# Chunked attention and a gated feed-forward block on one core: the query spread moves from GpSimd to VectorE, and GpSimd's loads get a small wait of their own

## The chip, the cores and the metric

The kernel runs on one core of a Trainium2 chip. The metric is the device time of one launch in microseconds, as the median of several runs. Four runs of the kernel before gave 236.3, 235.44, 234.52 and 234.93 us, median 235.18 us.

A core has five engines with instruction streams of their own: TensorE (PE in the profile) multiplies matrices into PSUM banks, VectorE (DVE) and ScalarE (ACT) do elementwise work, GpSimd (POOL) does elementwise work too and issues transfers, and SyncE (SP) issues transfers. Every stream runs in program order; an instruction that waits holds up all that stand behind it on its engine.

## The reference

Sequences of 768 tokens, 4 batches, 8 heads of 64. Each chunk of 32 queries attends to 8 memory rows, 16 keys to the left of the chunk, its own 32 and 8 to the right. Then a gated feed-forward layer over all 3072 tokens.

```python
for c in range(nc):                                   # 24 chunks of 32
    k_full = concat([mem_k, k[:, :, l_start:r_end]])  # up to 8 + 56 rows
    v_full = concat([mem_v, v[:, :, l_start:r_end]])
    a = softmax(scale * q_c @ k_full.T)
    out[:, :, c_start:c_end] = a @ v_full
x = out.transpose(0, 2, 1, 3).reshape(B * S, H * D)   # 3072 x 512
y = (maximum(x @ w_gate, 0) * (x @ w_val)) @ w_out    # 512 -> 1536 -> 512
```

## The kernel before

The tokens are worked in 8 blocks of 384 (`NB = 8`, `TB = 384`; block n is half a sequence). For a block there are two kinds of work.

**Attention, per pair of heads** (`hp`, 4 pairs, each 128 partitions wide). `score` (L282 for blocks 2 and later) multiplies the transposed keys `kT` with `qbd`, in which the transposed queries `qT` of the two heads of a pair are laid out block-diagonally: the two halves are copied into place and the rest stays zero. `score_exp` (L294) takes three exponentials on ScalarE. `step_v` (L344) multiplies with the value windows; `step_ln` (L350, two logarithms) and `step_e` (L355, one exponential) give the reciprocal of the row sums on ScalarE; `step_m` (L361, two multiplications on VectorE) writes the pair's part of `xT`.

**The feed-forward layer** of a block is 15 units: 12 inner units (`ffn_unit`, 4 matmuls into a bank `g_ps`, 4 into `v_ps`, L382; then a relu on ScalarE, L390, and a multiplication on VectorE, L394, after which the two banks are free) and 3 out units (`out_unit`, 12 matmuls into `o_ps`, L418; ScalarE copies the result and issues its store from block 2 on). Four PSUM banks (`fps`) go round among `g_ps`, `v_ps` and `o_ps`; so the units can run two ahead of the elementwise work. The scores have one buffer (`sps`), and `step_v` has one pair of banks (`xo_ps`, `xs_ps`).

`run(n, at)` is one round. It walks through the 15 units u of block n - 1 and puts block n's attention in between: pair hp's score goes behind unit `at[hp]`, its `step_v` and `step_ln` into the middle of unit `at[hp] + 2` with `step_e` behind that unit, and `step_m` ahead of unit `at[hp] + 3`. The list is (0, 3, 6, 9), but (3, 5, 8, 11) in the first round, which is `run(3)`. In `run(3)` units 0 and 1 are opened together (chunks). Everything is issued in the order written; there is no scheduler.

**Where the inputs come from.** For each block from 2 on, `loads(n)` has GpSimd issue 4 transfers for the key band, 4 for the queries (`q16n`) and 4 for the value band; SyncE copies the memory rows. SyncE then issues two transposing transfers, `turn_k_dma` (L233, `kT`) and `turn_q_dma` (L238, `qT`). Then `spread_q` (L246) makes `qbd` out of `qT` by four copies: two of 64 x 384 (pair 0, the two halves) and two of 64 x 1152 (pairs 1 to 3). `qbds` has two buffers, and so have `kT`, `qT`, `k16s`, `vwins` and `q16n`.

**Who does the spread, before.** For block 2 it is VectorE, ahead of the six out units in `run1()`. For block 3 it is GpSimd, in `run1()` behind the fourth of the six out units; for blocks 4 to 7 it is GpSimd too, issued in `run(n)` at u = 9 right behind the transposes. As `loads(n + 2)` stands behind `spread_q(n + 1)` in GpSimd's stream, the loads wait for that block's query transpose and for the four copies.

`gate` is a tile of 128 x 1. It is written once in the kernel before, by a GpSimd copy from `kTs[2]`, so that the loads of block 3, which stand behind it, wait for block 2's key transpose.

Of the kernel before, what the change touches and what calls it, by code (L numbers as in the profile page):

```python
# [17 lines left out]
def kernel(  # L18
# [12 lines left out]
    nc = tc.nc  # L31
# [5 lines left out]
    HP = H // 2  # L37
# [4 lines left out]
    NB = B * S // TB  # L42
    NQ = 4
# [7 lines left out]
    NDC = DFF // 128  # L51
    NT = TB // 128
# [20 lines left out]
    dve_copy, act_copy = nc.vector.tensor_copy, nc.scalar.copy  # L73
# [10 lines left out]
    qbds = [const.tile([128, NQ, HP, 2, QB], F16, name=f"qbd{p}") for p in range(2)]  # L84
# [12 lines left out]
    gate = const.tile([128, 1], F16, name="gate")  # L97
# [42 lines left out]
    def load_band(n, src_t, dsts):  # L140
        b, p = divmod(n, 2)
        for i in range(NQ):
            m0, m1 = (16 if (p == 0 and i == 0) else 0), (112 if (p == 1 and i == NQ - 1) else BAND)
            src = bass.AP(tensor=src_t.tensor, offset=src_t[b, 0, TB * p + QB * i - 16 + m0, 0].offset,
                          ap=[[D, m1 - m0], [S * D, H], [1, D]])
            pool_dma(dsts[p][NMEM + m0:NMEM + m1, i, :, 0:D], src)  # L146
# [6 lines left out]
    def load_mem_k(n):  # L153
        b, p = divmod(n, 2)
        m = memk[:, H * b:H * b + H, :]
        src = bass.AP(tensor=m.tensor, offset=m.offset, ap=[m.ap[0], [0, NQ], [1, H * D]])
        sp(k16s[p][0:NMEM].rearrange("m i h d -> m i (h d)"), src)

    def load_mem_v(n):
        b, p = divmod(n, 2)  # L160
        for i in range(NQ):
            sp(vwins[p][0:NMEM, i, :, 0:D], memv[:, H * b:H * b + H, :])
# [3 lines left out]
    def load_q_tokens(n):  # L166
        b, p = divmod(n, 2)
        q16s[n] = half.tile([QB, NQ, H, D], F16, tag="q16", name="q16n")
        for i in range(NQ):
            src = bass.AP(tensor=q.tensor, offset=q[b, 0, TB * p + QB * i, 0].offset,  # L170
                          ap=[[D, QB], [S * D, H], [1, D]])
            pool_dma(q16s[n][:, i], src)  # L172
# [6 lines left out]
    kTs, qTs = {}, {}  # L179
# [51 lines left out]
    def turn_k_dma(n):  # L231
        kTs[n] = turned.tile([128, NQ, HP, 128], F16, tag="kT", name="kT")
        nc.sync.dma_start_transpose(kTs[n].rearrange("p i a m -> p (i a) m"),  # L233
                                    k16s[n % 2].rearrange("p i h d -> p (i h d)"))

    def turn_q_dma(n):
        qTs[n] = turned.tile([128, NQ, HP, QB], F16, tag="qT", name="qT")
        nc.sync.dma_start_transpose(qTs[n].rearrange("p i a m -> p (i a) m"),  # L238
                                    q16s[n].rearrange("p i h d -> p (i h d)"))

    def spread_q(n, copy=nc.gpsimd.tensor_copy):

        for a in (slice(0, 1), slice(1, HP)):
            for hh in range(2):
                s = slice(D * hh, D * hh + D)
                copy(qbds[n % 2][s, :, a, hh, :], qTs[n][s, :, a, :])  # L246


    exs, lns, rinvs, xTs = {}, {}, {}, {}
# [108 lines left out]
    def step_m(n, hp):  # L358
        rinv = rinvs.pop((n, hp))
        for hh in range(2):  # L360
            nc.vector.tensor_tensor(out=x_of(n)[D * hh:D * hh + D, hp, :], in0=vbanks[n, hp][hh][0:D],  # L361
                                    in1=rinv[:, hh, :], op=ALU.mult)
# [5 lines left out]
    def ffn_open(n, ms, spare=False):  # L368
        if ms[0] == 0:
            gvs[n] = gpool.tile([128, NDC, TB], F16, name="gv")  # L370
        units[n] = []
        for m in ms:
            if spare:
                sc = pools["s"].tile([128, 2, 512], F32, tag="sc", name="gv_ps")
                pair = sc[:, 0, 0:TB], sc[:, 1, 0:TB]
            else:
                pair = bank("g_ps")[:, 0:TB], bank("v_ps")[:, 0:TB]
            units[n].append((pair, m))
# [17 lines left out]
    def ffn_close(n):  # L396
        for x in range(len(units[n])):
            ffn_relu(n, x)
            ffn_mult(n, x)
# [11 lines left out]
    def out_unit(n, t, between=()):  # L411
        o_ps = bank("o_ps")
        last = n == NB - 1 and t == NT - 1
        for m in range(NDC):
            if m == NDC // 2:
                for piece in between:
                    piece()
            nc.tensor.matmul(o_ps, lhsT=gvs[n][:, m, 128 * t:128 * t + 128], rhs=wo[:, m, :],  # L418
                             start=(m == 0), stop=(m == NDC - 1))
        o_sb = opool.tile([128, DM], F32, name="o_sb")  # L420
        row0 = TB * n + 128 * t
        if last:
            for s, copy, dma in ((slice(0, 256), dve_copy, sp), (slice(256, 512), act_copy, act_dma)):
                copy(o_sb[:, s], o_ps[:, s])
                dma(out[row0:row0 + 128, s], o_sb[:, s])
        elif n < 2:
            dve_copy(o_sb, o_ps)
            sp(out[row0:row0 + 128, :], o_sb)
        else:
            nc.scalar.copy(o_sb, o_ps)  # L430
            act_dma(out[row0:row0 + 128, :], o_sb)

    def unit(n, u, between=()):
        if u < NDC:
            ffn_unit(n, u, between)
        else:
            out_unit(n, u - NDC, between)
# [80 lines left out]
    def chunk(n, f):  # L518
        for x in range(2):
            for a in range(2):  # L520
                ffn_mm(n, x, f, a)
# [161 lines left out]
    def pieces(n, what):  # L683
        for w, hp in what:
            STEP[w](n, hp)
# [3 lines left out]
    def run(n, at):  # L689
        for u in range(NDC + NT):  # L690
            if n < NB:
                pieces(n, [("m", hp) for hp in range(HP) if u == at[hp] + 3])
            now = [hp for hp in range(HP) if n < NB and u == at[hp] + 2]
            inner, outer = ("ve", "") if u >= NDC else ("v", "e")
            if n == 3 and u < 2:

                if u == 0:
                    ffn_open(2, (0, 1))
                    for f in range(NFC):
                        chunk(2, f)  # L700
                    ffn_close(2)
            else:
                unit(n - 1, u, [lambda w=(w, hp): pieces(n, [w]) for hp in now for w in inner])
            pieces(n, [(w, hp) for hp in now for w in outer])
            if n < NB:
                pieces(n, [("s", hp) for hp in range(HP) if u == at[hp]])
            if u == 9 and n + 1 < NB:
                turn_k_dma(n + 1)
                turn_q_dma(n + 1)
                spread_q(n + 1)  # L710

    def pair2(hp):
        if hp < HP:
            score(2, hp)
        if hp > 0:
            step_v(2, hp - 1)
        if hp > 1:
            step_m(2, hp - 2)  # L720
        if hp < HP:
            score_exp(2, hp)
        if hp > 0:
            step_ln(2, hp - 1)
            step_e(2, hp - 1)

    def run1():
        for u in range(NDC):
            unit(1, u)
            if u < len(clear):  # L730
                clear[u]()
        spread_q(2, dve_copy)
        for t in range(2 * NT):
            out_unit(t // NT, t % NT, [lambda: pair2(t - 1)] if t > 0 else [])
            if t == 1:
                turn_k_dma(3)
            if t == 2:
                turn_q_dma(3)
            if t == 3:
                spread_q(3)  # L740
        step_m(2, HP - 1)

    def loads(n):
        if n < NB:
            load_mem_k(n)
            load_band(n, k, k16s)
            load_q_tokens(n)
            load_band(n, v, vwins)
            load_mem_v(n)


    nc.gpsimd.tensor_copy(gate, kTs[2][:, NQ - 1, HP - 1, 0:1])
    loads(3)
    run1()
    for n in range(2, NB):
        loads(n + 2)
        run(n + 1, (3, 5, 8, 11) if n == 2 else (0, 3, 6, 9))
# [1 line left out]
_INS = ['q', 'k', 'v', 'mem_k', 'mem_v', 'moe_w_gate', 'moe_w_val', 'moe_w_out']  # L759
_OUTS = [((3072, 512), 'float32')]  # L760
# [25 lines left out]
```

## Time and profile before

| what | value |
|---|---|
| median of four runs | 235.18 us (234.52 to 236.3) |
| device time of the profiled execution | 236.3 us |
| span of the profiled execution, first to last instruction | 234.3 us |
| granted TensorE clock, mean | 1.000 |
| TensorE matmuls busy | 225.9 us, 96% of the span |
| ScalarE, VectorE, GpSimd busy | 139.3, 110.7, 103.5 us |
| start-up until the first long chain of matmuls | some 25 us, bound by weight loads |
| six out units of blocks 0 and 1 with block 2's attention (`run1`) | 56.5 to 74.5 us |
| `run(3)`: block 2's units, block 3's attention | 74.5 to 101.9 us |
| `run(4)`, `run(5)`, `run(6)`, `run(7)`, then block 7's units | from 101.9, 128.6, 154.7, 180.7, 206.7 us |

The stages' bounds are the starts of the first matmuls of each block in the timeline of TensorE. In a row of the timeline the first two columns are the start and the duration of what is merged in the row, in microseconds; behind them stand the engine, the line, the operation, what it writes and reads, and the number of instructions; a bracket gives how long the engine was idle before, and what released it. Matmuls overlap: four with 384 columns are shown as 0.81 us long, while the next four start 0.65 us after them.

### The profile page before, as it was taken

What the parts mean: (1) busy time and instruction counts of PE and PEld (TensorE: products, weight loads), DVE (VectorE), ACT (ScalarE), POOL (GpSimd) and SP (SyncE); (2) the same over time, 40 slices, a digit from 0 to 9 for tenths busy, and PEclk for the clock granted to TensorE, in tenths of its full rate; (3) what the DMA queues carried; (4) which work ended last, traced back from release to release, by engine and by line L of the source; (5) the groups of instructions that cost most, each with busy time, mean ns of one, the idle gap of its engine ahead of it and who ended that gap; (6) DMA issues with size and microseconds to landing.
All of it is one profiled execution on the core that took longest, in us unless ns stands there. A gap on an engine that the chain in (4) does not pass through costs nothing.

```text
span 234.3 us, 4593 instructions
## 1 busy us (share of the span) xinstructions
PE 225.9 (96%) x1727; PEld 131.1 (56%) x1727; DVE 110.7 (47%) x214; ACT 139.3 (59%) x294; POOL 103.5 (44%) x140
## 2 busy tenths in 40 slices
PE   7999899999999999999999999999999999999993
PEld 3655455665554666446654666456654666456541
DVE  4685647883546445225461266215560365214300
ACT  3483793342397488657882798458873898433420
POOL 8778766431950598049803990795050000000000
PEclk9999999999999999999999999999999999999999
DMA  7999999999999899969998999299902100120012
GB/s 166 172 195 196 196 191 207 162 123 158 129 159 153 237 73 134 150 178 67 140 144 147 104 139 178 71 139 174 171 0 90 45 3 0 45 92 0 0 46 91
DMA packets 110144, 28.47 MB, mean 122 GB/s; under 512 B 93882, under 2 KB 107178, under 8 KB 110122
## 3 DMA queue, kind: packets, MB, share of 16 engines
q0 software_dynamic: 81760, 15.13, 81.1%
q1 hardware_dynamic: 25354, 8.07, 22.6%
q10 hardware_dynamic: 3008, 4.98, 6.0%
q8 instruction: 13, 0.21, 0.3%
q14 instruction: 9, 0.07, 0.1%
HBM read 31.08 MB, written 6.29 MB: 160 GB/s over the span
## 4 chain that ended last, share of the span: by engine, by line
PE 72%; DMA 19%; POOL 4%; ACT 1%; issue 1%; DVE 0%; SPq 0%; POOLq 0%
PE v_ps L382 22%; PE g_ps L382 22%; PE o_ps L418 20%; DMA qT<-q16n 7%; DMA wg<-in_moe_w_gate_dram 3%; DMA wv<-in_moe_w_val_dram 3%; DMA rk<-in_k_dram 3%; PE sc_ps L282 3%; DMA q16n<-in_q_dram 2%; POOL qbd L246 2%; POOL k L146 1%; PE xo_ps L344 1%; PE xs_ps L344 1%; POOL q16n L172 1%; ACT ex L294 1%
## 5 line engine op out<-in xcount | busy, mean ns | idle before, releaser
L394 DVE TENSOR_TENSOR gv<-v_ps,gr 128x384 f16<-128x384 f32 x95 | 52.5, 555 | 83.9 <-ACT gr L390 68.5
L382 PE MATMUL v_ps<-xT,wv 128*128 128x384 f16 x380 | 79.1, 326 | 0.8 <-DMA wv<-in_moe_w_val_dram 0.5
L382 PE MATMUL g_ps<-xT,wg 128*128 128x384 f16 x380 | 79.3, 326 | 0.3 <-DMA wg<-in_moe_w_gate_dram 0.2
L418 PE MATMUL o_ps<-wo,gv 128*128 128x512 f16 x288 | 64.3, 379 | 0.0
L390 ACT ACTIVATE gr<-g_ps 128x384 f16<-128x384 f32 x95 | 46.2, 489 | 28.9 <-PE g_ps L382 15.7
L382 PEld LDWEIGHTS <-wg 128*128 128x128 f16 x384 | 36.7, 98 | 23.8 <-issue 1.1
L382 PEld LDWEIGHTS <-wv 128*128 128x128 f16 x384 | 36.1, 98 | 22.9 <-DMA wv<-in_moe_w_val_dram 0.9
L418 PEld LDWEIGHTS <-gv 128*128 128x128 f16 x288 | 27.9, 98 | 31.7
L294 ACT ACTIVATE ex<-sc_ps,bias 128x256 f16<-128x256 f32 x84 | 33.4, 469 | 10.8 <-PE sc_ps L282 7.6
L246 POOL COPY qbd<-qT 64x384 f16<-64x384 f16 (+1 forms) x20 | 16.5, 825 | 48.4 <-DMA qT<-q16n 47.5
L430 ACT COPY o_sb<-o_ps 128x512 f32<-128x512 f32 x17 | 10.0, 586 | 27.9 <-PE o_ps L418 17.8
L146 POOL DMA_DIRECT2D k<-in_k_dram x24 | 21.5, 904 | 2.4 <-DMA wv<-in_moe_w_val_dram 1.0
L355 ACT ACTIVATE rinv<-ln,mln 64x768 f32<-64x768 f32 x24 | 22.2, 925 | 0.2
L146 POOL DMA_DIRECT2D vwin<-in_v_dram x24 | 21.5, 904 | 0.5 <-DVE gv L394 0.3
L172 POOL DMA_DIRECT2D q16n<-in_q_dram x24 | 18.5, 778 | 3.5 <-DMA wo<-in_moe_w_out_dram 3.5
L361 DVE TENSOR_TENSOR xT<-xo_ps,rinv 64x384 f16<-64x384 f32 x24 | 13.2, 550 | 11.7 <-ACT rinv L355 11.7
L350 ACT ACTIVATE ln<-xo_ps 64x384 f32<-64x384 f32 x24 | 11.7, 487 | 11.8 <-PE xs_ps L344 11.7
L361 DVE TENSOR_TENSOR xT<-xs_ps,rinv 64x384 f16<-64x384 f32 x24 | 13.2, 551 | 0.7
L344 PEld LDWEIGHTS <-vwin 128*128 128x128 f16 x192 | 10.8, 98 | 3.5 <-issue 0.4
L282 PE MATMUL sc_ps<-qbd,kT 128*128 128x192 f16 x96 | 11.8, 246 | 0.5 <-POOL qbd L246 0.5
L344 PE MATMUL xo_ps<-ex,vwin 128*128 128x96 f16 x96 | 11.1, 206 | 0.4 <-ACT ex L294 0.4
L350 ACT ACTIVATE ln<-xs_ps 64x384 f32<-64x384 f32 x24 | 11.4, 474 | 0.0
(92 smaller groups left out, 136.0 us busy)
## 6 DMA issues: line engine op xcount, KB each, us to landing
out_dram<-o_sb ACTq DMA_DIRECT2D x17, 256.0 KB
q16n<-in_q_dram POOLq DMA_DIRECT2D x24, 96.0 KB, 4.8
k<-in_k_dram POOLq DMA_DIRECT2D x18, 120.0 KB, 4.0
vwin<-in_v_dram POOLq DMA_DIRECT2D x18, 120.0 KB, 7.6
wg<-in_moe_w_gate_dram POOLq DMA_DIRECT2D x6, 256.0 KB, 8.1
wv<-in_moe_w_val_dram POOLq DMA_DIRECT2D x6, 256.0 KB, 8.9
wo<-in_moe_w_out_dram POOLq DMA_DIRECT2D x3, 512.0 KB, 10.8
out_dram<-o_sb SPq DMA_DIRECT2D x6, 256.0 KB
```

Of the source, the lines that this page charges most:

```text
L146: pool_dma(dsts[p][NMEM + m0:NMEM + m1, i, :, 0:D], src)
L172: pool_dma(q16s[n][:, i], src)
L246: copy(qbds[n % 2][s, :, a, hh, :], qTs[n][s, :, a, :])
L294: nc.scalar.activation(flat[:, :, :, s], view[:, :, :, s], ACT.Exp, scale=SCALE, bias=(bias1 if n == 1 else bias)[:, g:g + 1])
L344: nc.tensor.matmul((xo, xs)[hh][:, QB * i:QB * i + QB], lhsT=vw[:, i, 2 * hp + hh, :], rhs=ex[:, hh, i, :], start=True, stop=True)
L350: nc.scalar.activation(ln[:, hh], vbanks[n, hp][hh][D:128], ACT.Ln, scale=1.0 / 64.0)
L355: nc.scalar.activation(rinv, lns.pop((n, hp)), ACT.Exp, scale=-1.0, bias=mln64[0:D, :])
L361: nc.vector.tensor_tensor(out=x_of(n)[D * hh:D * hh + D, hp, :], in0=vbanks[n, hp][hh][0:D], in1=rinv[:, hh, :], op=ALU.mult)
L382: nc.tensor.matmul(ps[a], lhsT=(wg, wv)[a][:, f, 128 * m:128 * m + 128], rhs=xTs[n][:, f, :], start=(f == 0), stop=(f == NFC - 1))
L390: nc.scalar.activation(grs[n, m], g_ps, ACT.Relu)
L394: nc.vector.tensor_tensor(out=gvs[n][:, m, :], in0=v_ps, in1=grs.pop((n, m)), op=ALU.mult)
L418: nc.tensor.matmul(o_ps, lhsT=gvs[n][:, m, 128 * t:128 * t + 128], rhs=wo[:, m, :], start=(m == 0), stop=(m == NDC - 1))
```

## The change

VectorE does every spread. For block 3 it stands behind unit 3 of `run(3)`; for blocks 4 to 7 behind the last out unit (u = 14) of the round. Ahead of `loads(n + 2)` GpSimd gets a copy of one column of `qTs[n + 1]` into `gate`. In `run(3)` block 3's scores go behind units 4, 7, 9 and 11; `step_v`, `step_e` and `step_m` follow from that by the same offsets.

```diff
-    def spread_q(n, copy=nc.gpsimd.tensor_copy):
+    def spread_q(n):
         for a in (slice(0, 1), slice(1, HP)):
             for hh in range(2):
                 s = slice(D * hh, D * hh + D)
-                copy(qbds[n % 2][s, :, a, hh, :], qTs[n][s, :, a, :])
+                dve_copy(qbds[n % 2][s, :, a, hh, :], qTs[n][s, :, a, :])
...
             if u == 9 and n + 1 < NB:
                 turn_k_dma(n + 1)
                 turn_q_dma(n + 1)
+
+            if n == 3 and u == 3:
+                spread_q(3)
+            if u == NDC + NT - 1 and n + 1 < NB:
                 spread_q(n + 1)
...
-        spread_q(2, dve_copy)
+        spread_q(2)
...
             if t == 2:
                 turn_q_dma(3)
-            if t == 3:
-                spread_q(3)
...
     for n in range(2, NB):
+        if n + 2 < NB:
+            nc.gpsimd.tensor_copy(gate, qTs[n + 1][:, NQ - 1, HP - 1, 0:1])
         loads(n + 2)
-        run(n + 1, (3, 5, 8, 11) if n == 2 else (0, 3, 6, 9))
+        run(n + 1, (4, 7, 9, 11) if n == 2 else (0, 3, 6, 9))
```

## The prediction

> **What bounds the kernel now.** I read the page's busy times first, then the waits of TensorE, then the timelines of the stage that the change touches.
>
> ```profile
> span 234.3 us, 4593 instructions
> PE 225.9 (96%) x1727; PEld 131.1 (56%) x1727; DVE 110.7 (47%) x214; ACT 139.3 (59%) x294; POOL 103.5 (44%) x140
> ...
> PE sc_ps L282 <- POOL qbd L246: 0.5, 1, 0.5
> ...
> PE xo_ps L344 <- ACT ex L294: 0.4, 1, 0.4
> ```
>
> TensorE is busy for 225.9 of 234.3 us at a granted clock of 1.000, and the chain of waits is plain matmuls from 103.8 us to the end. The reader is to see how little TensorE waits: in the part that the change can reach there are two waits, one for GpSimd's `qbd` and one for an exponential. A gain can come from those two alone. Their true price is read from starts in TensorE's timeline, since four matmuls of 384 columns are followed 0.65 us after their start:
>
> ```profile
> 79.77 0.81 PE L382 MATMUL v_ps<-xT,wv 128*128 128x384 f16 x4
> 80.42 0.49 PE L282 MATMUL sc_ps<-qbd,kT 128*128 128x192 f16 x4
> 80.75 0.81 PE L382 MATMUL g_ps<-xT,wg 128*128 128x384 f16 x4
> ...
> 85.32 0.81 PE L382 MATMUL g_ps<-xT,wg 128*128 128x384 f16 x4
> 86.53 0.20 PE L344 MATMUL xo_ps<-ex,vwin 128*128 128x96 f16 x1 [0.40 <-ACT ex L294]
> ...
> 102.52 0.81 PE L382 MATMUL v_ps<-xT,wv 128*128 128x384 f16 x4
> 103.84 0.49 PE L282 MATMUL sc_ps<-qbd,kT 128*128 128x192 f16 x4 [0.52 <-POOL qbd L246]
> ```
>
> The value step of pair 1 could have started at 85.32 + 0.65 = 85.97 and started at 86.53: 0.56 us lost. Block 4's first score could have started at 103.17 and did at 103.84: 0.67 us lost. Together 1.23 us, 0.5% of the span. The same rows give the sizes used below: half a unit 0.65, a unit 1.30, a score 0.33 us; a value step takes 0.34 and an out unit 2.59 us by their starts.
>
> **The wait at 103.84, and what the spread costs on either engine.**
>
> ```profile
> 78.83 3.46 POOL L246 COPY qbd<-qT 64x384 f16<-64x384 f16 x4 [10.91 <-DMA qT<-q16n]
> 82.25 3.60 POOL L146 DMA_DIRECT2D k<-in_k_dram  x4
> ...
> 102.72 3.48 POOL L246 COPY qbd<-qT 64x384 f16<-64x384 f16 x4 [10.19 <-DMA qT<-q16n]
> 106.15 3.54 POOL L146 DMA_DIRECT2D k<-in_k_dram  x4
> ```
>
> ```profile
> 58.58 2.19 DVE L246 COPY qbd<-qT 64x384 f16<-64x384 f16 x4 [1.46 <-DMA qT<-q16n]
> ...
> 80.69 0.56 DVE L394 TENSOR_TENSOR gv<-v_ps,gr 128x384 f16<-128x384 f32 x1 [0.74 <-PE v_ps L382]
> ...
> 100.00 0.55 DVE L361 TENSOR_TENSOR xT<-xo_ps,rinv 64x384 f16<-64x384 f32 x1 [4.42 <-ACT rinv L355]
> 100.58 0.55 DVE L361 TENSOR_TENSOR xT<-xs_ps,rinv 64x384 f16<-64x384 f32 x1
> ```
>
> GpSimd's four copies take 3.46 us (two short ones of 0.505, two long ones of 1.144); VectorE did the same four for block 2 in 2.19 (0.255 and 0.794). GpSimd loses 5 x 4 copies, some 16.5 us, and gains four copies of one column at 0.19 us each (the one copy into `gate` in the trace took 0.188). Behind each of these stand only the next block's 12 loads on GpSimd, 4 x 0.904 + 4 x 0.778 + 4 x 0.904 = 10.3 us of issue; for those wait SyncE's two transposes, and for these the next spread. So block 4's loads start at 78.83 + 0.2 = 79.0 instead of 82.25, and `qT` of block 4, which let GpSimd go on at 102.72, can land 3.2 us earlier, at 99.5; at worst it lands where it did. SyncE's order of issues is not moved.
>
> The spread of block 4 now stands on VectorE behind pair 3's two multiplications, which ended at 101.13. With `qT` there at 99.5 the two short copies are done at 101.7; with `qT` still at 102.72, at 102.72 + 0.52 = 103.24. The score is wanted at 103.17, or a little later as below. So the 0.67 us go in either case, to 0.1.
>
> **Blocks 5 to 7.** VectorE is idle for 6.62 us behind pair 3's multiplications in each of these rounds (the idle time before its rows at 130.32 and 156.37), and 2.19 us of copies go there. GpSimd's spreads started at 126.45, 147.53 and 170.13 us, while the first scores stood at 129.89 and later: nothing waited before, and the earlier loads only add slack. Cost and gain are nothing. Without that cover, that is with `qT` landing inside the next round, VectorE would hold the multiplications of units 0 and 1, and 2.19 us would count; `qT` would have to land over 3 us later than now.
>
> **Block 3: the spread behind unit 3.** VectorE ends unit 3's multiplication at 81.25 (80.69 + 0.56), and `qT` of block 3 is there since 78.83, so the spread runs from 81.27 to 83.46. The first score now stands behind unit 4: TensorE wants it at 80.42 + 1.30 = 81.72, and its two short copies end at 81.8. With some 0.05 us of signalling (GpSimd's second short copy ended at 103.79, the score began at 103.84) it starts at 81.87: **0.15 us lost**, which is new. The bounds are 0 and, with GpSimd's 0.505 per copy, 0.65; I take VectorE's own row.
>
> Behind the copies stand the multiplications of units 4 and 5. Unit 4's ends at 83.46 + 0.56 = 84.02, and its bank is wanted next by unit 6's second half: score to 82.20, unit 5 to 83.50, half of unit 6 to 84.15, pair 0's value step to 84.49. Slack 0.47 us, no loss. Pair 0's value step is wanted at 84.15; its exponentials run from 82.40 to 83.60 (1.20 us, the row at 80.95 below): no loss.
>
> **Block 3: the new places (4, 7, 9, 11).** The wait at 86.53 has a pattern on ScalarE:
>
> ```profile
> 80.95 1.20 ACT L294 ACTIVATE ex<-sc_ps,bias 128x256 f16<-128x256 f32 x3 [0.49 <-PE sc_ps L282]
> ...
> 83.58 0.47 ACT L350 ACTIVATE ln<-xs_ps 64x384 f32<-64x384 f32 x1
> 84.08 0.49 ACT L390 ACTIVATE gr<-g_ps 128x384 f16<-128x384 f32 x1
> 84.47 0.92 ACT L355 ACTIVATE rinv<-ln,mln 64x768 f32<-64x768 f32 x1
> 85.30 1.18 ACT L294 ACTIVATE ex<-sc_ps,bias 128x256 f16<-128x256 f32 x3
> ```
>
> With scores at 3 and 5, pair 0's value step lies in unit 5 and pair 1's score behind the same unit 5. ScalarE then has two logarithms, a relu, the reciprocal and three exponentials in a row. From the start of one value step (82.70) to the next (86.53) that chain takes 3.83 us, while TensorE has 0.34 + 0.65 + 0.33 + 1.30 + 0.65 = 3.27 us of work: 0.56 lost. In the new list 4 and 7 don't collide. But the value steps fall in units 6, 9, 11 and 13, and scores behind units 9 and 11: pair 1's value step meets pair 2's score in unit 9, with the next value step again two units on. That is the same pattern, so **the 0.56 us are lost again, in unit 11**. The second meeting (unit 11) is followed by an out unit: 0.34 + 0.65 + 0.33 + 2.59 + 1.30 = 5.21 us of work against 3.83, no loss. Bounds for unit 11: 0, if relus and exponentials interleave better there, to 0.9, if pair 1's value step too runs out of its slack of 0.4.
>
> **The sum.** Lost before 0.56 + 0.67 = 1.23; lost after 0.15 + 0.56 = 0.71. Gain 0.5 us: the span of the profiled execution 234.3 would be 233.8, and its device time 236.3 would be 235.8. That execution lies 1.1 us above the median of the four, 2.0 us above its own span. From the median: 235.18 - 0.5 = **234.7 us**.
>
> One row speaks to a rule against moving copies to VectorE: block 2's four copies ran from 58.58 to 60.77 while GpSimd issued four loads (57.73, 3.58 us), and the same four took 3.60 and 3.54 us elsewhere without such copies. The Trainium skill (SBUF — State Buffer, "SBUF: two separate sides") says that a VectorE copy that takes both ports locks GpSimd out, so that it can't write the descriptors of its transfers meanwhile. By the rule up to 2.19 us of each block's earlier start would be given back; by the row nothing; TensorE's sum is 234.7 by both, as block 4's `qT` needs no earlier landing.
>
> **The rivals.**
> - *Both waits go.* ScalarE gets through unit 9 in time and the short copies are hidden. For it: 0.15 us is a guess of a few hundredths of signalling. Against it: the same chain is measured at 3.83 against 3.27. Gain 1.23: 234.0 us (235.18 - 1.2).
> - *The change does not reach the time.* The loads stay where they are since transfers, not issue, bound them, and what the scores lose in block 3 equals what block 4 gains: losses of 0.65 + 0.56 against 1.23 give 235.2 us. For it: the four loads of a band take 4 us to land whoever issues. Against it: the spread on VectorE removes 0.67 even with a late `qT`.
> - *Slower: VectorE's spread holds unit 4's multiplication and TensorE finds no bank in unit 6.* It decides once the four copies take over 2.66 us (2.19 + the slack of 0.47). With GpSimd's durations (3.46 us) the score loses 0.65, the bank another 0.3 (unit 4's multiplication ends at 85.29, the bank is wanted at 84.99), unit 11 0.56 to 0.9: 1.5 to 1.85 against 1.23, so 235.5 to 235.8 us. For it: the copies will run beside the loads and between multiplications. Against it: 2.19 us was measured beside loads as well.
>
> **How the numbers follow.** Forecast 0.52, both waits gone 0.20, no effect 0.10, slower 0.18. The known bounds give 234.0 to 235.5 for the forecast's mechanism (losses 0 + 0 to 0.65 + 0.9, against 1.23); runs of one kernel differ by more (234.52 to 236.3), so 0.3 us is added on each side: 233.7 to 235.8. 0.5% is 1.2 us, about what a measurement of this kernel can tell from no change. The forecast lies inside it; the rival without waits lies on its edge, and half of it with the forecast's upper tail makes 0.20 for faster; over half of the slower case, where further stalls would add to it, makes 0.11; 0.69 is left for the same.
>
> **What would show it.** Right: no wait of TensorE for `qbd` at block 4's first score; a short one (0.1 to 0.2 us) at block 3's first; a wait of about 0.5 us for an exponential at the value step in unit 11, some 92 us into the span; GpSimd's loads for block 4 from about 79 us; VectorE's spreads of about 2.2 us at 81.3 and 101.3; no TensorE wait in later rounds. Wrong: waits of TensorE for a bank in units 5 to 7 of `run(3)`, spreads of 3 us or more, or `qT` later than 102.7. More than 1.2 us of gain would need waits that this one execution doesn't show, such as a later `qT` in others.

## The result, and the profile after

The changed kernel takes 234.53 us (median of 53 runs, 233.72 to 235.72), the kernel before 235.23 (79 runs, 234.43 to 236.99). The ratio is 0.9968 with a 95% interval of 0.9960 to 0.9976: faster by 0.7 us, within the 0.5% that the prediction counted as no change. The forecast was 234.7 us. Medians here and below leave out the few executions that ran over 1.5% above the fastest of the same kernel.

Two of the waits of TensorE after the change (total, number, longest; of the rows left out one of 0.3 us, for a copy of an out unit, stands alike before and after, the others are of the start-up):

```profile
PE xo_ps L344 <- ACT ex L294: 0.4, 1, 0.4
...
PE sc_ps L282 <- DMA vwin<-memv: 0.2, 1, 0.2
```

The wait for `qbd` at block 4's first score is gone, the wait for an exponential is there, and a small new one stands at a score. TensorE's timeline gives their prices:

```profile
81.60 0.81 PE L382 MATMUL v_ps<-xT,wv 128*128 128x384 f16 x4
82.59 0.49 PE L282 MATMUL sc_ps<-qbd,kT 128*128 128x192 f16 x4 [0.18 <-DMA vwin<-memv]
...
92.06 0.81 PE L382 MATMUL g_ps<-xT,wg 128*128 128x384 f16 x4
93.27 0.20 PE L344 MATMUL xo_ps<-ex,vwin 128*128 128x96 f16 x1 [0.39 <-ACT ex L294]
...
103.39 0.81 PE L382 MATMUL v_ps<-xT,wv 128*128 128x384 f16 x4
104.04 0.49 PE L282 MATMUL sc_ps<-qbd,kT 128*128 128x192 f16 x4
```

Counted as in the prediction (four matmuls, 0.65 us): 82.59 - 82.25 = 0.34 us lost at block 3's first score, 93.27 - 92.71 = 0.56 at the value step in unit 11, and nothing at block 4's first score, where 103.39 + 0.65 is 104.04. That is 0.90 instead of 1.23 us. The bracket at 82.59 names a transfer of memory rows, which a score doesn't read; VectorE's second short copy ended at 82.54 (a single record), 0.05 us before the score, and it was the same to 0.02 us in the two later traces of this kernel. From `run(3)`'s first matmul (75.05, and 74.51 before) to block 4's first score it is 28.99 instead of 29.33 us: 0.34 gained. The rest of the 0.7 us must lie elsewhere, and this one execution doesn't show where: its start-up happened to be 0.54 us longer.

GpSimd and VectorE did what the diff says. GpSimd's timeline, with the new waits and the loads behind them:

```profile
79.50 0.19 POOL L759 COPY gate<-qT 128x1 f16<-128x1 f16 x1 [11.46 <-DMA qT<-q16n]
80.36 3.60 POOL L146 DMA_DIRECT2D k<-in_k_dram  x4 [0.67 <-issue]
...
99.45 0.19 POOL L759 COPY gate<-qT 128x1 f16<-128x1 f16 x1 [8.80 <-DMA qT<-q16n]
```

VectorE's spreads of blocks 3, 4 and 7:

```profile
81.70 2.55 DVE L246 COPY qbd<-qT 64x384 f16<-64x384 f16 x4
...
102.04 1.94 DVE L246 COPY qbd<-qT 64x384 f16<-64x384 f16 x4
...
176.02 1.51 DVE L246 COPY qbd<-qT 64x384 f16<-64x384 f16 x4
```

Block 4's query transpose let GpSimd go on at 99.45 instead of 102.72. Against the first matmul of `run(3)` that is 24.4 us instead of 28.2, but it varies: 24.5 to 28.2 us in the five traces of the runs below in which GpSimd makes the spread and no loads are delayed, 23.2 to 24.4 in six with the spread on VectorE and the waits into `gate`. The loads start 5.3 us into the round instead of 7.7, so 2.4 us earlier and not the 3.2 of the prediction: behind the small copy GpSimd is idle for 0.67 us. The four copies, the same work each time, take 2.55, 1.94 and 1.51 us; the last has no loads beside it.

### The profile page after: what moved, and what is told of

Same layout as the page of the kernel before. It is cut to its first block, busy times and chain, and to the rows that moved or that the text cites. A ratio compares the mean times of both kernels' runs of the same rounds, so it can differ in the third digit from the quotient of the medians.

```text
span 234.0 us, 4602 instructions
## 1 busy us (share of the span) xinstructions
PE 225.4 (96%) x1727; PEld 130.7 (56%) x1727; DVE 120.4 (51%) x234; ACT 139.5 (60%) x294; POOL 88.4 (38%) x124
## 3 DMA queue, kind: packets, MB, share of 16 engines
q1 hardware_dynamic: 25354, 8.07, 24.5%
## 4 chain that ended last, share of the span: by engine, by line
PE 84%; DMA 6%; POOL 5%; DVE 1%; ACT 1%; issue 1%; POOLq 0%; SPq 0%
PE o_ps L418 27%; PE v_ps L382 24%; PE g_ps L382 24%; DMA rq<-in_q_dram 4%; PE sc_ps L282 3%; PE xo_ps L344 2%; DMA vwin<-memv 2%; PE xs_ps L344 2%; POOL rk L131 1%; POOL wg L176 1%; POOL rv L499 1%; POOL rq L134 1%; DVE kq L219 1%; POOL rk L128 1%; PE xs_ps L311 0%
## 5 line engine op out<-in xcount | busy, mean ns | idle before, releaser
L759 POOL COPY gate<-qT 128x1 f16<-128x1 f16 x4 | 0.8, 188 | 42.5 <-DMA qT<-q16n 42.5
L246 DVE COPY qbd<-qT 64x384 f16<-64x384 f16 (+1 forms) x24 | 11.9, 495 | 1.8 <-DMA qT<-q16n 1.1
```

The source lines that it names most:

```text
L246: dve_copy(qbds[n % 2][s, :, a, hh, :], qTs[n][s, :, a, :])
```

## The experiments

All times are in us. "Outside" is the device time less the span, as the median over a kernel's runs; within a kernel it varies by 0.1 to 0.2, but for the kernel with late loads and the change (1.79 to 2.36). "Exit" is the stretch in the trace from the issue of the last store to the end of the span. The last three columns are TensorE's losses in rounds 3 and 4, counted as above, in the one trace of each kernel.

| kernel | ratio to before (95%) | median span | outside | exit | block 3's first score | value step | block 4's first score |
|---|---|---|---|---|---|---|---|
| before | 1 | 233.2 | 2.05 | 3.08 | 0 | 0.56 | 0.67 |
| before_2 | one run | 232.5 | 2.07 | 3.10 | 0 | 0.56 | 0 |
| changed | 0.9968 (0.9960 to 0.9976) | 232.8 | 1.71 | 2.64 | 0.34 | 0.56 | 0 |
| after_2 | one run | 232.6 | 1.70 | 2.65 | 0.44 | 0.56 | 0 |
| after_3 | 0.9976 (0.9960 to 0.9993) | 232.95 | 1.70 | 2.66 | 0.15 | 0.55 | 0 |
| places_only | 0.9993 (0.9964 to 1.0021) | 233.2 | 1.70 | 3.08 | 0 | 0.55 | 0 |
| spread_only | 0.9990 (0.9969 to 1.0011) | 232.9 | 2.02 | 2.66 | 0 | 0.56 | 0 |
| tail_gp | 0.9994 (0.9982 to 1.0007) | 233.35 | 1.69 | 3.08 | 0.43 | 0.55 | 0 |
| tail_act | 0.9988 (0.9971 to 1.0004) | 233.1 | 1.72 | 3.09 | 0 | 0.55 | 0.20 |
| before_exits | 0.9973 (0.9957 to 0.9990) | 232.65 | 1.73 | 2.65 | 0 | 0.56 | 0 |
| split_places | 0.9941 (0.9926 to 0.9956) | 232.0 | 1.69 | 2.64 | 0 | 0 | 0 |
| no_gate | 0.9975 (0.9959 to 0.9991) | 232.85 | 1.69 | 2.66 | 0.42 | 0.56 | 0 |
| late_before | 1.0279 (1.0229 to 1.0329) | 240.45 | 2.03 | 2.65 | 0 | 0.55 | 6.93 |
| late_after | 1.0010 (0.9976 to 1.0045) | 233.7 | 2.29 | 2.66 | 0.57 | 0.55 | 2.23 |

**Are the two traces typical?** Both kernels, unchanged, once more.

> The kernel before, unchanged, for a second trace. If the two traces at hand are typical, TensorE loses 0.56 us at pair 1's value step (unit 7) and 0.67 us at block 4's first score again, 1.23 in all, to 0.1 us. If the traces understate the gain (0.34 us between 74.5 and 104 us there, 0.70 between the medians), the wait at block 4's first score is larger here, 1 us or more, because the query transpose of block 4 lands at another time after the start of its round.

> The changed kernel, unchanged, for a second trace. If the first is typical: 0.34 us lost at block 3's first score, 0.56 at the value step in unit 11, none at block 4's first score. If the first trace understates the gain, the loss at block 3's first score is smaller here, 0.2 us or less, with a first short copy on VectorE of 0.25 instead of 0.55 us.

For the kernel before neither expectation came out. GpSimd's spread for block 4 and that block's first score in the second trace of before:

```profile
97.96 3.47 POOL L246 COPY qbd<-qT 64x384 f16<-64x384 f16 x4 [8.06 <-DMA qT<-q16n]
```
```profile
102.07 0.41 PE L282 MATMUL sc_ps<-qbd,kT 128*128 128x192 f16 x3
```

The second row, from TensorE's timeline, has no bracket: no wait. The transpose landed 4.8 us earlier than in the first trace, more than the 1.1 us by which the whole round was earlier, so that the 0.67 us, on which most of the forecast stood, were a feature of one execution. The changed kernel's losses are the same to 0.1 us. By these second traces rounds 3 and 4 lose 0.56 before and 1.00 after the change: the change would make the kernel slower by 0.44 us. It did not, so something outside these rounds had to pay.

**The places, or the spread?** One of each alone:

```diff
# places_only, against before
-        run(n + 1, (3, 5, 8, 11) if n == 2 else (0, 3, 6, 9))
+        run(n + 1, (4, 7, 9, 11) if n == 2 else (0, 3, 6, 9))
# spread_only, against the changed kernel
-            if n == 3 and u == 3:
+            if n == 3 and u == 2:
...
-        run(n + 1, (4, 7, 9, 11) if n == 2 else (0, 3, 6, 9))
+        run(n + 1, (3, 5, 8, 11) if n == 2 else (0, 3, 6, 9))
```

> The kernel before with block 3's scores behind units 4, 7, 9, 11 and nothing else. My theory: the places only move the wait of 0.56 us from unit 7 to unit 11, and the 0.67 us at block 4's first score stay, so the ratio to before is 1.000, between 0.9985 and 1.0015. Rival, that the places bring the gain: a ratio of 0.997 to 0.998 and no wait of over 0.2 us in unit 11.

> The changed kernel with the old places 3, 5, 8, 11 and, so that it is ahead of the first score, block 3's spread behind unit 2. My theory: block 4's first score waits no more (0.67 us gained), the 0.56 us in unit 7 stay, and block 3's first score waits 0.2 to 0.5 us behind VectorE's short copies: a ratio of 0.998 to 0.9995. Rival, that spread and loads bring the whole gain of 0.7 us: 0.997 or less. Rival, that the places bring it: 1.000 or more.

Both medians lie about where my theory had them, and both intervals are too wide to say more. In each the trace has one loss alone, the 0.56 us at a value step; the loss that I expected behind unit 2 in spread_only is not there (its two short copies took 0.24 and 0.26 us). What told more were the two columns beside it, which I had taken for constants. With the new places alone the time outside the span falls from 2.05 to 1.70. With the spread alone the exit falls from 3.08 to 2.66. The changed kernel has both.

**The exit.** The last stores are issued in the same way in both kernels (ScalarE's timeline, the first kernel before, the second changed; the spans end at 234.25 and 234.01):

```profile
231.17 0.34 ACTq L425 DMA_DIRECT2D out_dram<-o_sb  x1
```
```profile
231.37 0.34 ACTq L425 DMA_DIRECT2D out_dram<-o_sb  x1
```

The changed kernel issues its last store 0.20 us later and ends 0.24 earlier. GpSimd's last records in the trace, which the timeline leaves out (the trace's names, start and duration), show where:

```
               before        changed       tail_gp       before_exits
semaphore      233.15 0.02   233.35 0.02   232.53 0.02   232.66 0.02
drain          233.53 0.24   233.43 0.10   232.90 0.24   232.74 0.10
range clear    233.80 0.14   233.56 0.14   233.17 0.14   232.87 0.14
drain          233.98 0.05   233.73 0.05   233.35 0.05   233.04 0.05
```

From the last semaphore to the clearing of the range it is 0.65 us before and 0.21 after the change; everything else is equal. GpSimd's program is 16 instructions shorter in the changed kernel (185 records instead of 201), and ScalarE's is 2 longer (441 instead of 439: with the new places it needs two more semaphore waits). So the lengths were tried alone:

```diff
# tail_gp, against the changed kernel
+        if n == 5:
+            for _ in range(16):
+                nc.gpsimd.memset(gate, 0.0)
         loads(n + 2)
# tail_act, against before (pad is a new tile of 128 x 1)
             if u < len(clear):
                 clear[u]()
+            if u in (2, 3):
+                nc.scalar.copy(pad, mln64)
```

> The changed kernel with 16 fills of one column into gate on GpSimd, ahead of block 7's loads, where GpSimd waits anyway. It has then as many instructions on GpSimd as the kernel before (201 in the trace instead of 185), and no spread. Theory: the changed kernel gains at its exit, since GpSimd's shorter program needs no further instruction fetch for its last drain; with the 16 fills that drain starts 0.3 us later and takes 0.24 instead of 0.10 us, the stretch from the last store's issue to the end of the span grows from 2.65 to 3.1 us, and the ratio to before rises from 0.997 to 0.9985 or more. Rival, that the copies themselves or the work in rounds 3 and 4 make the difference: the exit stays at 2.65 us and the ratio at 0.997.

> The kernel before with two copies of one column on ScalarE in block 1's inner units, where it is idle; nothing else. ScalarE has then at least 441 instructions in the trace instead of 439, as many as with the new places. Theory: the device time outside the span is 2.05 us with 439 and 1.70 with 441 by where ScalarE's program ends, so it falls to 1.70 us here, the span stays, and the ratio to before is 0.998 to 0.999. Rival, that the new places as such shorten it: 2.05 us outside the span, ratio 1.000.

Both did what the theory says of the times. 16 small fills give the changed kernel its long exit back (3.08, the drain as in the third column above) and its ratio goes to 0.9994. They stand behind the wait for the transpose and hold block 7's loads up by 2.6 us, but no wait of TensorE follows. Two copies of one column on ScalarE take 0.33 us off the time outside the span. The rivals are out by these two columns; the ratio of tail_act alone, whose interval includes 1.000, would not tell. Then both lengths were changed in the kernel before, with nothing of the change:

```diff
# before_exits, against tail_act
+        if n == 5:
+            for _ in range(7):
+                nc.gpsimd.memset(gate, 0.0)
         loads(n + 2)
```

> The kernel before with nothing of the change, but with programs of other lengths: 7 fills of one column on GpSimd ahead of block 7's loads (208 of its instructions in the trace, the length at which the kernel with late loads had its short exit) and two copies of one column on ScalarE (441, as in the changed kernel). Theory: the changed kernel's gain lies in its exit and not in rounds 3 and 4, so this one takes 2.65 us from the last store's issue to the end of the span and 1.70 us outside it and gains the same: ratio to before 0.996 to 0.9975. Rival, that the gain needs the spread on VectorE or the new places: 0.9985 or more.

> The changed kernel, unchanged, on the same chip as before_exits. Theory: ratio to before 0.996 to 0.9976 as recorded, equal to that of before_exits within 0.0015; 2.65 us from the last store's issue to the end of the span, 1.70 us outside it. Rival: at least 0.002 below before_exits.

The ratios are 0.9973 and 0.9976 on the same chip. A kernel that does nothing of the change gains as much as the changed one. GpSimd has 207 records here, more than the 201 of the kernel before, and its exit is short: it isn't the shorter program as such that gains. Of the fourteen traces the five with 201 records have the long exit, the nine with 180, 185, 191, 207 or 208 the short one. Why some lengths cost 0.44 and 0.35 us more is not shown here. A fetch of instructions at the program's end would fit in part: in the five traces with the long exit, and in no other, a single packet of 8 KB on a queue that the profile calls "instruction" starts between 0.02 us before the end of the span and 0.24 behind it (at 234.23 in the kernel before). But it starts 0.4 us or more after the late drain has ended, so it isn't what the drain waited for. Nor does ScalarE's length alone set the time outside the span: late_after has 441 records and 2.29 us, the one kernel where it varied much from run to run.

**What the late transpose is worth.** Seven fills of a spare tile ahead of block 4's loads, in both kernels (5.5 us of GpSimd's time before, 5.9 in the changed one):

```diff
+        if n == 2:
+            for _ in range(7):
+                nc.gpsimd.memset(pad, 0)
         loads(n + 2)
```

> The kernel before with seven fills of a spare tile (128 x 768 words, some 0.75 us each) on GpSimd ahead of block 4's loads, so that they and block 4's query transpose come some 5.2 us later. My theory: TensorE's wait at block 4's first score is set by that transpose, which left 0 to 3 us of room before (waits of 0.67, 0, 0 and 0.20 us in four traces); it grows to 2 to 6 us here, and the ratio to before is 1.008 to 1.025. Rival, that the wait has another cause: below 0.7 us, ratio 1.000 to 1.002.

> The changed kernel with the same seven fills ahead of block 4's loads. My theory: its loads start some 3.2 us earlier and its short copies are 0.5 us quicker, so the same delay leaves a wait of 0 to 2 us at block 4's first score, 3 to 4 us less than in the kernel before with the fills; ratio to before 0.997 to 1.006. Rival, that the changed kernel has no more room for a late transpose: the same wait as there, ratio 1.005 or more above.

Block 4's spread and first score, in the kernel before with the fills and in the changed one with them (the spare tile's line moves the others down by one):

```profile
108.15 3.46 POOL L247 COPY qbd<-qT 64x384 f16<-64x384 f16 x4 [10.82 <-DMA qT<-q16n]
```
```profile
109.26 0.80 PE L283 MATMUL sc_ps<-qbd,kT 128*128 128x192 f16 x4 [6.77 <-DMA out_dram<-o_sb]
```
```profile
105.53 1.75 DVE L247 COPY qbd<-qT 64x384 f16<-64x384 f16 x4 [3.57 <-DMA qT<-q16n]
```
```profile
106.22 0.49 PE L283 MATMUL sc_ps<-qbd,kT 128*128 128x192 f16 x4 [2.06 <-DVE qbd L247]
```

The bracket at 109.26 names a store, which a score doesn't read; GpSimd's second short copy ended at 109.21 (a single record). The wait is 6.93 against 2.23 us by the starts, both more than I expected, and so is the ratio of 1.0279. The difference of 4.7 is more than the 3.7 that I put down to earlier loads and quicker copies. Against the time at which the score was wanted (102.33 and 104.00) the loads (87.01 and 85.12) start 3.6 us earlier, the transpose lands 0.7 us sooner behind them, and the copies give 0.4. The trace of the changed one is of a longer execution, 236.4 us of span where the median is 233.7; but the medians of the span, 240.45 and 233.7, lie further apart than the spans of the two traces, 241.2 and 236.4. The mechanism of the prediction stands: the landing of block 4's transpose sets this wait, and the changed kernel has several microseconds more room. It just seldom needs them: in the five traces with GpSimd's spread and no added delay the wait was 0.67, 0, 0, 0.20 and 0 us.

**Are the waits into `gate` needed?** The changed kernel without them:

```diff
-        if n + 2 < NB:
-            nc.gpsimd.tensor_copy(gate, qTs[n + 1][:, NQ - 1, HP - 1, 0:1])
         loads(n + 2)
```

> The changed kernel without the four copies into gate, so that each block's loads start as soon as their buffers are free. Theory: the loads of block 4 then run beside block 3's transposes, block 3's query transpose lands later than 79.5 us, and TensorE waits at block 3's first score, some 1 to 4 us more than the 0.34 to 0.44 us in the changed kernel; later blocks lose nothing. Rival, that the wait is needless: block 3's transpose lands as before and the time is that of the changed kernel to 0.2%.

Half of it came. VectorE's spread of block 3, which now waits for the transpose:

```profile
81.64 1.75 DVE L246 COPY qbd<-qT 64x384 f16<-64x384 f16 x4 [0.30 <-DMA qT<-q16n]
```

The transpose lands some 2.5 us later against the round's start (81.6 less 74.6, instead of 79.5 less 75.05); the loads of block 4 now start at 67.64, beside it, and it is issued 1.1 us later in the round. But the first score now stands behind unit 4, and the time is that of the changed kernel: 0.9975. With these places the wait is not needed. The 0.42 us lost at that score are of another kind than in the changed kernel: here the transpose is late, and the short copies take 0.25 and 0.26.

**A version that loses nothing in these rounds.** Pair 0's short copies go behind units 0 and 1, which are opened together, the long ones stay behind unit 3 (`spread_q` takes the parts as a second argument), and the places are those where a score meets the previous pair's value step in unit 11 alone:

```diff
-            if n == 3 and u == 3:
-                spread_q(3)
+            if n == 3 and u == 1:
+                spread_q(3, (slice(0, 1),))
+            if n == 3 and u == 3:
+                spread_q(3, (slice(1, HP),))
...
-        run(n + 1, (4, 7, 9, 11) if n == 2 else (0, 3, 6, 9))
+        run(n + 1, (3, 6, 9, 11) if n == 2 else (0, 3, 6, 9))
```

> The changed kernel with block 3's spread split, pair 0's two short copies behind units 0 and 1 and the two long ones behind unit 3, and with the places 3, 6, 9, 11, so that a value step and the next pair's score meet in unit 11 alone, which an out unit follows. My theory: both remaining waits of rounds 3 and 4 go (0.34 to 0.44 at the first score, 0.56 at a value step), the span's median falls from 232.8 to 231.9, and the ratio to before is 0.994 to 0.996 if the time outside the span is 2.05 us, as ScalarE's program is then as long as before. Rival, that TensorE's waits don't set the end: 0.997 or more.

The ratio is 0.9941 (0.9926 to 0.9956), 233.68 us: faster than both kernels, and the only one whose rounds 3 and 4 have no loss. The span's median is 232.0 (231.9 expected). ScalarE's program has 441 records here, contrary to what I had assumed, and the time outside is 1.69.

## Why the prediction was right, and where it was not

Direction and size came true, and most of the steps; but the step that carried the gain failed, and another gain of the same size, which the prediction did not have, stood in its place. That the number was right is luck.

- **Block 4's first score, 0.67 us.** The wait goes, as forecast, and for the reason given (late_before and late_after). Its size failed: it was read from one execution, and over five traces it is 0.17 us on average.
- **Block 3's first score, 0.15 us.** Mis-sized. It is 0.34, 0.44 and 0.15 in three traces of the changed kernel and 0.43 in tail_gp, each time some 0.05 us behind the end of VectorE's second short copy. In the first trace the first short copy took 0.55 us instead of 0.25 (single records of the trace); in the second the other one took 0.67. I had taken VectorE's row of 58.58, whose short copies happened to fall inside one of GpSimd's issues, but for the first 0.06 us.
- **Unit 11, 0.56 us.** Right to the hundredth, place and cause: a score behind the same unit as a value step, with the next value step two units on. split_places, which keeps them apart, does away with it.
- **VectorE in unit 6.** No wait of TensorE for a bank; but the copies took 2.55 us in the first trace, and the slower rival had 2.66 as its point of decision.
- **Blocks 5 to 7, and GpSimd's loads.** No cost and no gain, as forecast: TensorE has no loss there in any trace. SyncE's queue and the loads behind the new wait cost nothing.
- **The sum.** "2.0 us above its own span" was taken as a constant, and so was the end of the span. Both depend on the kernel. Of the 0.70 us between the medians 0.34 lie outside the span (2.05 to 1.71) and 0.44 in the exit (3.08 to 2.64). The work in between got no faster: 0.70 - 0.78 leaves a loss of 0.1, and the losses say the same, 0.56 + 0.17 before and 0.56 + 0.31 (the mean of 0.34, 0.44 and 0.15) after, 0.14 more. TensorE's own stretch agrees: from the first out unit's first matmul to the start of the last matmul it is 172.33 us in split_places, without losses, and in every other trace without late loads this plus the losses of the table, to 0.07 us (173.60 and 172.93 in the two of the kernel before; 173.27, 173.36 and 173.07 in those of the changed one).

The rule on the port that VectorE and GpSimd share was weighed as up to 2.19 us lost by GpSimd. The trace of the changed kernel shows the time lost on the other side: GpSimd's four loads at 80.36 took 3.60 us beside the copies, as they did without, while VectorE's copies took up to 2.55 instead of 1.51.

## What to carry to other kernels

A wait of half a microsecond read in one execution is not yet a gain: a second trace of the same kernel shows whether it is there each time. When a gain is a few tenths of a percent, compare the exit and the time outside the span first; here engines' programs of another length gave 0.35 and 0.44 us, without touching the work. In a hand-written order, look for two long tasks that meet on one engine in one slot, and check the slot after the move as well as the one before.

## What the runs showed of the hardware

- The end of a kernel costs more or less with the length of the engines' programs: from GpSimd's last semaphore to the clearing of the range it is 0.65 us with 201 records and 0.21 with the others, and the time outside the span is 2.05 us with 439 records of ScalarE and 1.70 with 441, but for late_after. Only lengths that occurred in these kernels were tried.
- VectorE's copies of 16-bit data from SBUF to SBUF take longer across the end of one of GpSimd's issues of loads. Single records of the changed kernel's trace: short copies 0.25 us, but 0.41 to 0.60 where GpSimd goes from one load to the next under them; long ones 0.45 with no load beside them or inside one issue, 0.65 to 0.87 across such a boundary. In each case the slowed copy ends 0.05 to 0.09 us (short) or 0.25 to 0.30 us (long) behind the end of that load, as if it waited for it. In other traces a short copy whose first 0.17 us or less met the end of a load took 0.25 all the same. The key and value loads keep some 0.9 us each. The Trainium skill (SBUF — State Buffer, "SBUF: two separate sides") has the shared port pair as a lock that the first one holds for its whole instruction, with the other blocked. That fits these traces in part only: GpSimd is the first here and VectorE the one that loses, but copies inside one issue are not held up, and the port itself isn't seen in a trace.
- A long wait of TensorE costs beyond itself. In the kernel before with late loads the granted clock falls in the wait of 6.77 us that ends at 109.26 (page, 40 slices of 6.0 us, tenths):

```profile
PEclk9999999999999999986999999999999999999999
```

  By windows it was 0.75 from 105 to 108 us and 0.50 from 108 to 113, though TensorE was at work again from 109.26. From the first out unit's first matmul to the last matmul that trace is 8.9 us longer than the second trace of before (181.84 and 172.93), of which the wait itself is 6.9; some 2 us are left, and the starts of the matmuls behind the wait give them: 0.26, 0.63, 0.63 and 0.46 us more than at the full clock. The Trainium skill (TensorE: Matmul & The Clock Gate, "What's actually happening") has the clock halve after an idle window of about 3.4 us; the 0.50 here agrees.
